# An attention, router and gated-MLP kernel: exponentials and split remainders issued at another point of the attention tick

## The chip, the cores and the metric

The kernel runs on one core of a Trainium2 chip. The metric is the device time of one execution in microseconds (us), lower is better. Three runs of the kernel before took 2026.89 to 2027.23 us, their median is 2026.97 us.

## What is computed

The reference chains three layers; the change lies in the first one.

```python
scores = scale * np.matmul(q, k.transpose(0, 1, 3, 2))
mask = block_i >= block_j
scores = np.where(mask, scores, -1000000000.0)
scores = scores - np.max(scores, axis=-1, keepdims=True)
attn = np.exp(scores)
attn = attn / (np.sum(attn, axis=-1, keepdims=True) + 1e-09)
return np.matmul(attn, v)
...
x = _moe_ref(x=x, **moe_kwargs)
return _moe2_ref(x=x, **moe2_kwargs)
```

q, k and v are (4, 8, 576, 64): four batches of eight heads, 576 positions, 64 channels, with a mask over blocks of 64 positions. Its output, 2304 rows of 512, passes through eight experts with a router that is balanced in eight rounds, and then through a gated layer of width 1536.

## The kernel before, in words

**Pairs and ticks.** Two heads are worked on together, which makes 16 pairs, numbered 0 to 15. Each pair takes eight ticks (u = 0 to 7). A tick handles one piece of the masked score matrix: ticks 0 and 1 hold two row blocks of 64 each, ticks 2 to 5 one block with 320, 384, 448 and 512 columns, and ticks 6 and 7 the two halves (288 columns each) of the last block. So a score tile can be told by its width in the trace. The generator `attention` writes all ticks out in order, and each engine executes its own instructions in exactly that order; an instruction that waits holds up all that stand behind it on its engine or queue.

**One tick.** It has three thirds that end in a `yield`. The first third runs the events that are due in this tick (loads, maxima, scales and splits of coming pairs) and then the score matmuls of the tick (TensorE, L979 and L990). The middle third transposes probabilities that are four ticks old (TensorE, L1068 and L1077), normalises those that are two ticks old (`normalise`: two small VectorE operations that write r, L1035 to L1040, and a product on GpSimd, L1045), copies the transposes out (ScalarE, L1071 and L1078), and takes the row maxima of the tick (`maxima`, VectorE, L1003, which write bias). The last third does the value product at u = 4 and its copy to xf (ScalarE, L1110), the remaining transpose at u = 3, and then the exponentials of the tick before (`exps`, ScalarE, L1020, which write e and need bias).

At each `yield` the caller may put in a step of other work: the loading and splitting of expert weights (wr, w; L372, L377, L179, L183) and, after pair 3, the first part of the expert layer (`fill`: TensorE matmuls of L548 and L614 and their copies). That work fills TensorE beside attention.

**Splitting q and k.** From pair 4 on q and k are split into two float16 parts. For pair p, with r = 8p the tick at which it starts, `load_qk` (L911) brings q (i = 0) and k (i = 1) in, `max_qk` (L924) and `scale_qk` find a power of two, `hi_qk` (ScalarE, L941) writes the upper part into hl at ticks r - 6 (q) and r - 4 (k), and `lo_qk` (VectorE, L945) writes the remainder into hl at ticks r - 5 and r - 4. `lo_qk` also issues eight transfers on SyncE's queue (SP) from hl into st, four for q (L956) and four for k (L958). The scores of the pair's first tick need all eight.

**Buffers.** There is one buffer for q and one for k (qk). `load_qk` of pair p + 1 stands at ticks r - 6 and r - 5, so it waits on SP for the remainders of pair p, which are the last to read the buffer. Score tiles rotate through three PSUM banks, which the exponentials free.

Of the kernel before, what the change touches and what calls it, by code (L numbers as in the profile page):

```python
# [30 lines left out]
def attention_moe_glu_kernel(  # L31
# [74 lines left out]
    def across_mid(g):  # L106
        bank, g["free"] = spread[0](g["name"])
        n = g["n"]
        g["row"] = bank[:, : n * P].rearrange("p (n q) -> p n q", n=n)
        nc.tensor.matmul(  # L110
            bank[:, : n * P], ones, g["d"].rearrange("p n q -> p (n q)"), start=True, stop=True
        )
# [401 lines left out]
    behind = deque()  # L514
# [314 lines left out]
    NTK = len(TICKS)  # L829
# [5 lines left out]
    def attention(actx):  # L835
# [29 lines left out]
        def where(p):  # L865
            return p // NPAIR, ORDER[p % NPAIR]
# [3 lines left out]
        def load_v(b, hp, tag, bufs=1):  # L870
            t = tag
            if isinstance(tag, str):
                t = ap.tile([P, NJ, P], F32, tag=tag, name=f"{tag}_{b}_{hp}", bufs=bufs)
            cols = slice(hp * P, (hp + 1) * P)
            nc.gpsimd.memset(t[S - nf * P :, nf], 0.0)
            nc.sync.dma_start(t[:, :nf], v[b, : nf * P, cols].rearrange("(j p) d -> p j d", p=P))
            nc.sync.dma_start(t[: S - nf * P, nf], v[b, nf * P :, cols])
            return t
# [64 lines left out]
        def lo_qk(p, i):  # L943
            hl = st[p]["hl", i]
            nc.vector.scalar_tensor_tensor(  # L945
                hl[:, 1], qk.pop((p, i)), st[p]["s"][:, i : i + 1], hl[:, 0], op0=ALU.mult, op1=ALU.subtract
            )
            shape = [P, 2, S] if i == 0 else [P, 2, 2, S]
            t = ap.tile(shape, F16, tag=f"st{i}", name=f"st{i}_{p}", bufs=2)
            st[p]["qs" if i == 0 else "ks"] = t  # L950
            for h in range(2):
                a = slice(h * D, (h + 1) * D)
                for half in range(2):
                    d = slice(half * D, (half + 1) * D)
                    if i == 0:
                        nc.sync.dma_start(t[d, h], hl[a, half])  # L956
                    else:
                        nc.sync.dma_start(t[d, h], hl[a])  # L958

        def scores(p, u):  # L960
            g = st[p]
            if u == 0:
                for x in ("bias", "sum", "r"):
                    g[x] = small.tile([P, NC + 1], F32, tag=x, name=f"{x}_{p}")
            if (p, u) in shared:
                sp = shared.pop((p, u))
            elif u == NTK - 1:
                sp = ps_x.tile([P, 512], F32, tag="x", name=f"s_{p}_{u}")
            else:
                sp = ps_s.tile([P, 512], F32, tag="s", name=f"s_{p}_{u}")  # L970
            col, places = 0, []
            for c, k0, k1 in TICKS[u]:
                ps = sp[:, col : col + k1 - k0]
                col += k1 - k0
                places.append((c, k0, k1, ps, c if k0 == 0 else NC))
                if p < DIRECT:
                    for h in range(2):
                        a = slice(h * D, (h + 1) * D)
                        nc.tensor.matmul(  # L979
                            ps[h * CB : (h + 1) * CB],  # L980
                            g["q"][a, c * CB : (c + 1) * CB],
                            g["k"][a, k0:k1],
                            start=True,
                            stop=True,
                        )
                    continue
                qs, ks = g["qs"], g["ks"]
                for i in range(2):
                    for h in range(2):
                        nc.tensor.matmul(  # L990
                            ps[h * CB : (h + 1) * CB],
                            qs[:, h, c * CB : (c + 1) * CB],
                            ks[:, h, i, k0:k1],
                            start=i == 0,
                            stop=i == 1,
                        )
            g["places", u] = places

        def maxima(p, u):
            g = st[p]  # L1000
            for c, k0, k1, ps, m in g["places", u]:
                k, to = k1 - k0, NC if u == NTK - 2 else c
                nc.vector.tensor_tensor_reduce(  # L1003
                    junk[:, :k],
                    ps,
                    zero.to_broadcast([P, k]),
                    g["nsc"],
                    g["bias"][:, NC : NC + 1] if u == NTK - 1 else 3.0e38,
                    ALU.add,
                    ALU.min,  # L1010
                    g["bias"][:, to : to + 1],
                )

        def exps(p, u):
            if u == NTK - 2:
                return
            g = st[p]
            for w in (u,) if u < NTK - 1 else (u - 1, u):
                for c, k0, k1, ps, m in g.pop(("places", w)):
                    nc.scalar.activation(  # L1020
                        et[c][:, k0:k1],
                        ps,
                        AF.Exp,
                        bias=g["bias"][:, c : c + 1],
                        scale=g["sc"],
                        accum_out=g["sum"][:, m : m + 1],
                    )
# [134 lines left out]
        def work(n):  # L1162
            for _ in range(min(n, len(pend))):
                pend.popleft()()

        def hurried():
            if hurry[0]:
                work(1)
                hurry[0] -= 1
                if not hurry[0]:  # L1170
                    ready[0] += S // 2

        events = {}

        def at(tick, f, *a):
            events.setdefault(tick, []).append(lambda: f(*a))

        for p in range(1, npairs):
            r = p * NTK
            if p < DIRECT:  # L1180
                if p > 1:
                    at(r - NTK, load_direct, p)
                    at(r - 2, lambda p: vt.update({p: load_v(*where(p), "v", 2)}), p)
                continue
            for i in range(2):
                if p > 1:
                    at(r - 14 + 1 * i, load_qk, p, i)
                at(r - 11 + i, max_qk, p, i)
                at(r - 6 + 2 * i, hi_qk, p, i)
                at(r - 5 + 1 * i, lo_qk, p, i)  # L1190
            at(r - 8, lambda p: across_mid(st[p]["m"]), p)
            at(r - 7, scale_qk, p)
            at(r - 2, lambda p: vt.update({p: load_v(*where(p), "v", 2)}), p)
        for b in range(B):
            r = (b - 1) * NPAIR * NTK
# [4 lines left out]
            r = r + NPAIR * NTK if b else NPAIR  # L1200
# [13 lines left out]
        def on(k):  # L1214
            return 0 <= k < tot

        for tk in range(tot + NTK):
            p, u = divmod(tk, NTK)
            calm[0] = 0 < u < 5
            here[0] = (p, u) if on(tk) else None  # L1220
            for f in events.pop(tk, ()):
                f()
            here[0] = None
            if on(tk):
                scores(p, u)
            if u == 6 and p < npairs:
                take(p, 0, values(p, 0))
            hurried()
            yield
            out1 = None  # L1230
            if on(tk - 4):
                out1 = transposes(*divmod(tk - 4, NTK))
            if hurry[0]:
                hurried()
            else:
                work(2 if len(pend) > 6 else 1)
            if on(tk - 2):
                normalise(*divmod(tk - 2, NTK))
            if out1:
                out1()  # L1240
            if on(tk):
                maxima(p, u)
            yield

            if p and u == 4:
                work(len(pend))
                take(p - 1, 1, values(p - 1, 1))
                st.pop(p - 1)
                vt.pop(p - 1)
                if p == npairs:  # L1250
                    work(len(pend))
                    ready[0] = B * S // 2
                elif p % NPAIR == 0:
                    hurry[0] = len(pend)
            if p and u == 3:
                rest(p - 1)()
            if on(tk - 1):
                exps(*divmod(tk - 1, NTK))
            if u != 4:
                hurried()  # L1260
            yield
# [647 lines left out]
```

## Time and profile before

| | |
|---|---|
| median of three runs | 2026.97 us |
| profiled execution | 2023.13 us, of which the span is 2021.3 us |
| TensorE busy | 1939.9 us (96%) |
| VectorE, ScalarE, GpSimd busy | 1587.4, 1400.9, 637.2 us |
| attention | from the start to about 345 us of the span |

Times in rows are microseconds from the span's start. PE is TensorE's matmul, PEld its weight load, DVE is VectorE, ACT is ScalarE, POOL is GpSimd, SPq is SyncE's queue of DMA issues. A row of the timeline gives start, length, engine, source line, operation, tiles and count; in square brackets stands how long the engine was idle before it, and what ended that. In a row of waits stand the waiting engine, tile and line, whom it waited for, the sum in us, how often, and the longest.

### The profile page before, as it was taken

What the parts mean: (1) busy time and instruction counts of PE and PEld (TensorE: products, weight loads), DVE (VectorE), ACT (ScalarE), POOL (GpSimd) and SP (SyncE); (2) the same over time, 40 slices, a digit from 0 to 9 for tenths busy, and PEclk for the clock granted to TensorE, in tenths of its full rate; (3) what the DMA queues carried; (4) which work ended last, traced back from release to release, by engine and by line L of the source; (5) the groups of instructions that cost most, each with busy time, mean ns of one, the idle gap of its engine ahead of it and who ended that gap; (6) DMA issues with size and microseconds to landing.
All of it is one profiled execution on the core that took longest, in us unless ns stands there. A gap on an engine that the chain in (4) does not pass through costs nothing. (4 is left out here: it accounts for less than half of the span.)

```text
span 2021.3 us, 47085 instructions
## 1 busy us (share of the span) xinstructions
PE 1939.9 (96%) x18378; PEld 1668.1 (83%) x18378; DVE 1587.4 (79%) x3360; ACT 1400.9 (69%) x2911; POOL 637.2 (32%) x904
## 2 busy tenths in 40 slices
PE   7789999999999999999999999999999989999998
PEld 3457677889888988878888898898889878888987
DVE  8986774888889788797978889788886787677766
ACT  6766775477777778777877877778776666544443
POOL 5644444013333333333333333333332342000000
PEclk9899999999999999999999999999999999999999
DMA  5333331327787786777767767777787200301112
GB/s 154 110 111 111 110 89 39 135 55 140 150 178 157 146 172 130 167 154 162 169 135 164 155 142 173 136 162 156 148 174 167 58 23 17 95 1 45 41 43 53
DMA packets 169615, 238.82 MB, mean 118 GB/s; under 512 B 16688, under 2 KB 85424, under 8 KB 169392
## 3 DMA queue, kind: packets, MB, share of 16 engines
q0 software_dynamic: 68288, 110.39, 31.6%
q1 hardware_dynamic: 100528, 124.90, 19.9%
q8 instruction: 144, 2.36, 0.5%
q14 instruction: 79, 0.65, 0.1%
q10 hardware_dynamic: 576, 0.53, 0.1%
HBM read 90.39 MB, written 24.38 MB: 57 GB/s over the span
## 5 line engine op out<-in xcount | busy, mean ns | idle before, releaser
L548 PEld LDWEIGHTS <-w 128*128 128x128 f16 x6720 | 607.4, 98 | 81.8 <-issue 18.4
L658 PEld LDWEIGHTS <-m_h 128*128 128x128 f16 x5292 | 513.8, 98 | 70.5 <-issue 6.8
L1538 POOL DMA_DIRECT2D acc<-ev x362 | 317.0, 924 | 585.8 <-ACT ev L1542 398.6
L548 PE MATMUL abc_m_b<-xs,w 128*128 128x256 f16 (+1 forms) x3840 | 472.5, 262 | 8.9 <-ACT m_t L575 5.3
L658 PE MATMUL m_o_b<-w,m_h 128*128 128x256 f16 x3024 | 404.3, 273 | 10.0 <-ACT ev L1542 6.1
L658 PE MATMUL m_o_ac<-w,m_h 128*128 128x256 f16 x2268 | 310.4, 273 | 0.0
L548 PE MATMUL abc_m_c<-xs,w 128*128 128x256 f16 (+1 forms) x1920 | 227.2, 262 | 0.0
L1542 ACT ACTIVATE ev<-m_o_b,pe 128x256 f32<-128x256 f32 x370 | 170.8, 479 | 70.7 <-PE m_o_b L658 49.3
L1542 ACT ACTIVATE ev<-m_o_ac,pe 128x256 f32<-128x256 f32 x236 | 136.2, 580 | 44.4 <-PE m_o_ac L658 43.0
L183 DVE SCALAR_TENSOR_TENSOR w<-wr,ws,w 128x512 f16<-128x512 f32 x210 | 156.0, 752 | 8.3 <-ACT w L179 8.3
L179 ACT ACTIVATE w<-wr,ws 128x512 f16<-128x512 f32 x210 | 150.1, 723 | 17.5 <-DVE ws L164 11.9
L194 DVE TENSOR_TENSOR m_h<-m_t,m_h 128x512 f16<-128x512 f32 x189 | 129.5, 686 | 34.3 <-ACT m_h L698 33.3
L698 ACT CAST m_h<-m_t 128x512 f16<-128x512 f32 x189 | 117.2, 620 | 26.6 <-DVE m_t L722 25.5
L691 ACT ACTIVATE m_h<-m_t 128x512 f16<-128x512 f32 x189 | 118.5, 627 | 22.4 <-DVE m_t L587 14.7
L1525 POOL DMA_DIRECT2D acc<-ev_s x52 | 62.1, 1194 | 222.1 <-ACT ev_s L1518 213.8
L695 DVE SCALAR_TENSOR_TENSOR m_h<-m_t,m_h 128x512 f16<-128x512 f32 x189 | 129.0, 687 | 3.1 <-ACT m_h L691 2.8
L548 PEld LDWEIGHTS <-gg_w 128*128 128x128 f16 x1260 | 114.3, 98 | 19.8 <-issue 7.7
L548 PEld LDWEIGHTS <-gv_w 128*128 128x128 f16 x1260 | 114.7, 98 | 15.2 <-issue 3.3
L1045 POOL TENSOR_SCALAR e<-e,r 128x64 f32<-128x64 f32 (+2 forms) x144 | 85.5, 600 | 120.1 <-DVE r L1040 84.5
L658 PEld LDWEIGHTS <-g_h 128*128 128x128 f16 x1134 | 110.5, 98 | 14.8 <-issue 1.9
L548 PE MATMUL abc_m_a<-xs,w 128*128 128x256 f16 (+1 forms) x960 | 118.7, 263 | 0.0
L1732 POOL TENSOR_TENSOR g_t<-v_t,g_t 128x512 f32<-128x512 f32 (+1 forms) x15 | 17.5, 1164 | 280.2 <-DVE v_t L572 239.7
(319 smaller groups left out, 3435.2 us busy)
## 6 DMA issues: line engine op xcount, KB each, us to landing
acc<-ev POOLq DMA_DIRECT2D x362, 256.0 KB, 4.1
wr<-in_w_dram SPq DMA_DIRECT2D x128, 256.0 KB, 5.4
acc<-ev_s POOLq DMA_DIRECT2D x52, 256.0 KB, 3.9
st<-hl SPq DMA_DIRECT2D x48, 144.0 KB, 3.4
raw_g<-in_w_gate_dram SPq DMA_DIRECT2D x12, 512.0 KB, 5.2
raw_v<-in_w_val_dram SPq DMA_DIRECT2D x12, 512.0 KB, 4.9
raw_o<-in_w_out_dram SPq DMA_DIRECT2D x12, 512.0 KB, 5.3
scr_g<-gg SPq DMA_DIRECT2D x21, 256.0 KB, 2.7
```

The lines of the kernel that those rows point to most:

```text
L179: nc.scalar.activation(hi, src, AF.Copy, scale=s)
L183: nc.vector.scalar_tensor_tensor(lo, src, s, hi, op0=ALU.mult, op1=ALU.subtract)
L194: nc.vector.tensor_sub(lo, src, hi)
L548: nc.tensor.matmul(ps[:, f, to : to + w], W[o][:, sh, k, f * P : (f + 1) * P], xs[:, o, mh, k, c0 : c0 + w], start=x not in begun, stop=Tr ...
L658: nc.tensor.matmul(ps, h[o][:, sh, k, ii * P : (ii + 1) * P], W[o][:, mh, k], start=o in (X11, X12) and k == 0 and j == 0, stop=True, skip ...
L691: nc.scalar.activation(hi, src, AF.Relu)
L695: nc.vector.scalar_tensor_tensor(lo, src, 0.0, hi, op0=ALU.max, op1=ALU.subtract)
L698: nc.scalar.copy(hi, src)
L1045: nc.gpsimd.tensor_scalar(et[c][:, :n], et[c][:, :n], g["r"][:, c : c + 1], 1.0, op0=ALU.mult, op1=ALU.mult)
L1525: nc.gpsimd.dma_start(acc[:, x - 1 : x + 1, cols], e, accum_op=ALU.add)
L1538: nc.gpsimd.dma_start(acc[:, x], e, accum_op=ALU.add)
L1542: nc.scalar.activation(e[:, cols], ps, AF.Copy, scale=p)
```

## The change

Two groups of calls are issued at another point of the tick. The exponentials of the tick before now stand at the end of the middle third, behind the row maxima, instead of in the last third. The remainders `lo_qk` stand at the end of the middle third of their tick, behind the row maxima and ahead of the exponentials, instead of among the events of its first third. No operation is added or left out.

```diff
-        events = {}
+        events, behind = {}, {}
...
                 at(r - 11 + i, max_qk, p, i)
                 at(r - 6 + 2 * i, hi_qk, p, i)
-                at(r - 5 + 1 * i, lo_qk, p, i)
+                behind.setdefault(r - 5 + i, []).append(lambda p=p, i=i: lo_qk(p, i))
...
             if on(tk):
                 maxima(p, u)
+            for f in behind.pop(tk, ()):
+                f()
+            if on(tk - 1):
+                exps(*divmod(tk - 1, NTK))
             yield
...
             if p and u == 3:
                 rest(p - 1)()
-            if on(tk - 1):
-                exps(*divmod(tk - 1, NTK))
             if u != 4:
                 hurried()
             yield
```

TensorE and GpSimd keep their order. Three places show what moves on the others.

VectorE, ticks 3 and 4 of pair 8, before (L945 writes the remainders of pair 9, the ISA rows are row maxima):

```order
L945 SCALAR_TENSOR_TENSOR hl_9_2404<-qk_9_2024,qk_s,hl_9_2404 128x576
L116 TENSOR_REDUCE v_r<-v_a 128x1
...
L1003 ISA junk,bias_2304<-s_3_2463,zero,sc_1980 128x384
L1003 ISA bias_2304 128x1
L945 SCALAR_TENSOR_TENSOR hl_9_2512<-qk_9_2056,qk_s,hl_9_2512 128x576
L1039 TENSOR_SCALAR r_2306<-sum_2305 128x1
L1040 RECIPROCAL r_2306<-r_2306 128x1
L1003 ISA junk,bias_2304<-s_4_2520,zero,sc_1980 128x448
```

and with the change:

```order
L116 TENSOR_REDUCE v_r<-v_a 128x1
...
L1003 ISA junk,bias_2304<-s_3_2457,zero,sc_1980 128x384
L1003 ISA bias_2304 128x1
L945 SCALAR_TENSOR_TENSOR hl_9_2404<-qk_9_2024,qk_s,hl_9_2404 128x576
L1039 TENSOR_SCALAR r_2306<-sum_2305 128x1
L1040 RECIPROCAL r_2306<-r_2306 128x1
L1003 ISA junk,bias_2304<-s_4_2514,zero,sc_1980 128x448
L1003 ISA bias_2304 128x1
L945 SCALAR_TENSOR_TENSOR hl_9_2512<-qk_9_2050,qk_s,hl_9_2512 128x576
```

Both remainders moved behind the row maxima of their tick.

SyncE's queue at the same place, before (qk_10 are the loads of pair 10, st_9 the transfers of pair 9, vs a load of v, y a store of the expert layer):

```order
L911 DMA qk_10_2406<-in_qT_dram 128x576
L1403 DMA y_86<-y_2373 128x512
L956 DMA st_9_2438<-hl_9_2404 64x576 x4
L911 DMA qk_10_2443<-in_kT_dram 128x576
L876 DMA vs_0_2459<-in_v_dram 128x4x128
L877 DMA vs_0_2459<-in_v_dram 64x128
L958 DMA st_9_2515<-hl_9_2512 64x1152 x4
```

and with the change:

```order
L911 DMA qk_10_2406<-in_qT_dram 128x576
L1405 DMA y_86<-y_2373 128x512
L911 DMA qk_10_2437<-in_kT_dram 128x576
L876 DMA vs_0_2453<-in_v_dram 128x4x128
L877 DMA vs_0_2453<-in_v_dram 64x128
L956 DMA st_9_2489<-hl_9_2404 64x576 x4
L958 DMA st_9_2530<-hl_9_2512 64x1152 x4
```

The load of the next pair's k, which waits for this pair's second remainder, now stands ahead of the four transfers of q. It is so at each of the eleven pairs 4 to 14; after pair 15 nothing is loaded.

ScalarE, ticks 2 to 5 of pair 1, before (e are exponentials, told by their width; w an expert weight; xf the copy of the value product):

```order
L1078 COPY a_0_278<-t_7_381 128x4x128
L179 ACTIVATE w_0_0_392<-wr_0_00_211,ws_0_371 128x512
L1078 COPY a_0_278<-t_r 128x128
L1020 ACTIVATE e_135,sum_323<-s_2_359,bias_322 128x320
L179 ACTIVATE w_0_1_401<-wr_0_10_215,ws_0_371 128x512
L1071 COPY a_1_403<-t_0_404 128x256
L1110 ACTIVATE xf_0_1_423<-x_1_412,vs_255 128x320
L1020 ACTIVATE e_137,sum_323<-s_3_378,bias_322 128x384
```

and with the change:

```order
L1078 COPY a_0_278<-t_7_381 128x4x128
L1020 ACTIVATE e_135,sum_323<-s_2_359,bias_322 128x320
L179 ACTIVATE w_0_0_393<-wr_0_00_212,ws_0_371 128x512
L1078 COPY a_0_278<-t_r 128x128
L179 ACTIVATE w_0_1_401<-wr_0_10_216,ws_0_371 128x512
L1071 COPY a_1_403<-t_0_404 128x256
L1020 ACTIVATE e_137,sum_323<-s_3_378,bias_322 128x384
L1110 ACTIVATE xf_0_1_424<-x_1_413,vs_255 128x320
```

The exponentials of 320 and 384 columns passed the instructions that stood between the copy of the transposes and them.

## Rows read from the trace of the kernel before

**Rows 1.** The page, busy time by engine.

```profile
PE 1939.9 (96%) x18378; PEld 1668.1 (83%) x18378; DVE 1587.4 (79%) x3360; ACT 1400.9 (69%) x2911; POOL 637.2 (32%) x904
```

**Rows 2.** Windows: stretch, length, busy time of each engine, PEclk, DMA share, GB/s.

```profile
0.00:56.00 56.00, 44.27 (x291) 22.03 (x292) 46.63 (x180) 36.43 (x107) 29.70 (x76) 1.00 0.48 144
56.00:150.00 94.00, 75.65 (x601) 47.09 (x600) 83.10 (x278) 67.25 (x175) 49.06 (x100) 0.89 0.39 112
150.00:345.00 195.00, 188.99 (x1761) 137.76 (x1760) 128.87 (x472) 130.59 (x347) 90.37 (x200) 1.00 0.32 91
```

**Rows 3.** Waits of DVE from 56 to 150 us: sum, times, longest.

```profile
DVE hl L945 <- ACT hl L941: 1.7, 2, 1.5
DVE w_(0, 1)_1828 L183 <- ACT w_(0, 1)_1828 L179: 1.2, 1, 1.2
```

**Rows 4.** Waits of DVE from 150 to 345 us.

```profile
DVE hl L945 <- ACT hl L941: 17.3, 8, 3.9
```

**Rows 5.** Waits of DVE from 0 to 56 us.

```profile
DVE r L1039 <- ACT e L1020: 2.4, 2, 1.4
```

**Rows 6.** Timeline of PE, score tile of tick 4 of pair 10.

```profile
216.53 0.57 PE L990 MATMUL s<-st,st 128*64 128x448 f16 x4 [0.80 <-ACT e L1020]
```

**Rows 7.** Timeline of SPq and DVE around the transfers of pair 4.

```profile
62.03 0.35 SPq L911 DMA_DIRECT2D qk<-in_kT_dram  x1
62.18 0.60 DVE L1003 CUSTOM_DVE_ANT_0 junk<-s,zero 128x448 bf16<-128x448 f32 x1
...
64.85 2.42 SPq L372 DMA_DIRECT2D wr<-in_w_dram  x4
...
69.87 0.68 DVE L377 TENSOR_REDUCE wmx<-wr 128x1 f32<-128x512 f32 x1
```

**Rows 8.** Tile wr, issue to landing: loads at 64.85, then at 109.03.

```profile
DMA to landing us min/median/max: 3.8/4.4/4.9
...
DMA to landing us min/median/max: 3.4/4.6/4.7
```

**Rows 9.** Timeline of SPq and DVE around the transfers of pair 6.

```profile
104.84 0.67 DVE L1003 CUSTOM_DVE_ANT_0 junk<-s,zero,sc 128x448 bf16<-128x448 f32 x1
...
106.59 2.39 SPq L958 DMA_DIRECT2D st<-hl  x4
109.03 2.52 SPq L372 DMA_DIRECT2D wr<-in_w_dram  x4
...
112.67 0.68 DVE L377 TENSOR_REDUCE wmx<-wr 128x1 f32<-128x512 f32 x1
```

**Rows 10.** Timeline of SPq, DVE and PE around the transfers of pair 9.

```profile
176.78 2.40 SPq L956 DMA_DIRECT2D st<-hl  x4
...
181.28 0.82 DVE L945 SCALAR_TENSOR_TENSOR hl<-qk,qk_s,hl 128x576 f16<-128x576 f32 x1 [3.85 <-ACT hl L941]
...
183.55 2.73 SPq L958 DMA_DIRECT2D st<-hl  x4
...
189.73 0.36 PE L990 MATMUL qk_a<-st,st 128*64 128x64 f16 x7 [0.33 <-DMA st<-hl]
```

**Rows 11.** Tile st, pair 9: issues (ns min/median/max, first and last start), landing.

```profile
L958 SPq DMA_DIRECT2D st<-hl x4: 587/602/807, 183.6 to 185.7; - x4
...
DMA to landing us min/median/max: 3.2/3.9/4.0
```

**Rows 12.** Timeline of PE, first scores of pair 13.

```profile
276.25 0.36 PE L990 MATMUL qk_a<-st,st 128*64 128x64 f16 x8
```

**Rows 13.** Tile st, pair 13: issues and landing, as in rows 11.

```profile
L958 SPq DMA_DIRECT2D st<-hl x4: 461/600/606, 269.4 to 271.2; - x4
...
DMA to landing us min/median/max: 3.5/3.9/4.0
```

**Rows 14.** Waits of PE from 56 to 150 us.

```profile
PE t L1077 <- POOL e L1045: 6.8, 4, 2.3
PE s L990 <- ACT e L1020: 6.5, 4, 2.6
```

## Prediction

> **What bounds the kernel now.** I read the page first: TensorE is busy for 96% of the span [rows 1], so a change can only win what TensorE loses somewhere, and attention is where it loses it. The busy times by stretch [rows 2] cut attention into three stages. From 0 to 56 us and from 56 to 150 us VectorE sets the pace: it is busy for 46.6 of 56 us and 83.1 of 94 us, while TensorE has 11.7 and 18.4 us idle. From 150 to 345 us TensorE sets the pace: 189.0 of 195 us busy, 6 us idle, VectorE at 128.9. So I count in two currencies. In the first two stages a microsecond counts if VectorE loses or gains it; in the third, if TensorE does. After 345 us nothing is moved, and the work left over is TensorE's, so what attention gains or loses goes into the end.
>
> Next I read who waits for whom on these two engines, and then the timeline of SyncE's queue beside it, since the moved remainders issue transfers.
>
> **What the change takes away.** PE's and POOL's orders stay as they are, and no operation comes or goes. Four waits can shrink.
>
> First, a remainder waits on VectorE for its upper part, which ScalarE writes in the same tick. In the second stage that is 1.7 us [rows 3]. Behind the row maxima the upper part has a third of a tick more, so I take all 1.7. The 17.3 us of the third stage [rows 4] I cost at nothing: TensorE's own work covers them, and they would count only if VectorE became the bound there.
>
> Second, the normalisation waits on VectorE for exponentials, 2.4 us in the first stage [rows 5]. There the exponentials of 320 and 384 columns pass an expert weight and the copy xf, so I take all 2.4.
>
> Third, in the second stage VectorE waits 1.2 us for an upper half of an expert weight [rows 3]. ScalarE reaches it sooner, because the exponentials of 384 columns now run while it would be waiting for the value product. I take 1.2.
>
> Fourth, in the third stage TensorE waits 0.8 us for exponentials to free a score bank [rows 6]; those pass a step of expert work. I take 0.8.
>
> The sum is 1.7 + 2.4 + 1.2 + 0.8 = 6.1 us. The lower bound of each is zero: an in-order engine that skips one wait may meet the next.
>
> **What the change adds.** The remainders issue eight transfers, and their place on SyncE's queue changes with them. The load of the next pair's k stands at the head of that queue until the second remainder has been read; the four transfers of q were ahead of it and are now behind it. Those four take 2.40 us of the queue [rows 10], which before ran in the wait between the two remainders. So the transfers of k, and what follows them, come 2.4 us later, plus whatever the second remainder itself is late. I follow it where something is waiting.
>
> Pair 4. The load of k went out at 62.03, right behind the second remainder. That remainder now ends where the row maxima ended before, since it leaves their front and goes to their back: 62.18 + 0.60 and about 0.1 for the read-out, 62.8. Then come the load (0.35), 2.4 and 2.4 for the eight transfers, and the four expert-weight loads start at 68.1 in place of 64.85, 3.2 us later [rows 7]. The shortest landing of those four was 3.8 us [rows 8], so the first was there at about 68.7, and VectorE read it at 69.87 [rows 7], 1.2 us later. 3.2 - 1.2 = 2.0 us of VectorE. With the longest landing, 4.9 us, nothing of the slack is left and it is 3.1. I take 2.0, because the first of four loads meets the least company.
>
> Pair 6. The maxima of tick 4 end at 104.84 + 0.67 = 105.5, and there the second remainder ends now. With 0.4 for the load and 4.8 for the transfers the weight loads start at 110.7 in place of 109.03, 1.7 us later [rows 9]. With the shortest landing, 3.4 us [rows 8], the slack before VectorE's read at 112.67 was 0.2. That leaves 1.5 us.
>
> The first scores of pairs 4 to 6 will also find their transfers late, and there TensorE waits, but VectorE, which sets the pace, comes to their maxima some microseconds after. I cost these at nothing; if that cover fails it is up to 1 us for each of the three.
>
> Pair 9, in the third stage. The second remainder is bound by the upper part, not by its place: it waited 3.85 us for it [rows 10], and the maxima that now go ahead fit into that wait. So it is not late, and the shift is the 2.4 us of q's transfers alone. The last of k's transfers was issued at 185.7 and the longest landing was 4.0 us [rows 11], which gives 189.7, and the scores started at 189.73 after a wait for just that [rows 10]. No slack: 2.4 us of TensorE.
>
> Pair 13. The last issue at 271.2 and 4.0 us to land [rows 13] give 275.2. The scores started at 276.25 [rows 12], a slack of 1.05: 2.4 - 1.05 = 1.35 us of TensorE.
>
> The other pairs of the third stage leave more between last issue and scores. I put them at zero, and keep up to 1 us for each of pairs 10, 11, 14 and 15.
>
> The sum is 2.0 + 1.5 + 2.4 + 1.35 = 7.25 us.
>
> On the landing the trace and the notes differ. The transfers of k, 144 KB each, took 3.2 to 4.0 us at pair 9 [rows 11]. The Trainium skill, "DMA: Bandwidth & Descriptors", section "Anatomy of one DMA", fits 2.0 us and bytes at 436 GB/s for a transfer that GpSimd issues, which for these would be an estimate of 2.3 us. By that, 1.7 us more slack, pair 13 would lose nothing, pair 9 about 0.7, the weights about 0.8 and 0.7, and the whole change would come out at about -3.9 us. The measured landing decides, and the sum stays on it.
>
> **Sum.** -6.1 + 7.25 = +1.15 us. Against the profiled execution's 2023.1 us that is 2024.3; the median of the runs lies 3.8 us above that execution, so I forecast **2028.1 us**, no change. With the gains halved or the losses halved, the forecast itself runs from 2024.5 to 2031.2. A difference of 0.2%, 4 us, is about what a measurement of this kernel can tell from no change.
>
> **The rivals.**
>
> *Late transfers everywhere (slower).* The load of k at the head of the queue delays the scores at all pairs of the third stage, not at two. The price is 2.4 + 1.35 for pairs 9 and 13 and 1 us each for the four others, 7.75, with 3.5 for the weights, and only half the gains, 3.0: +8.2 us, 2035. It decides from the point where the last transfer of k is issued less than about 6.4 us before the scores (4.0 us to land and the shift of 2.4). For it: pair 9 already waited for such a transfer. Against it: in every other pair there was no wait at all for them. Every such gap also sits in the stage in which the granted clock was 1.00, full 2.4 GHz; in the stage before, with TensorE busy for 80%, it was 0.89 [rows 2], which means that some of it ran at 1.2 GHz. A gap that takes the clock down would add to the price.
>
> *The exponentials are the chain (faster).* In the second stage TensorE waits 6.8 us for normalised rows and 6.5 us for exponentials [rows 14]. If these chains, and not VectorE's work, set the pace there, then earlier exponentials shorten them, by half at a guess: -6.6 us on top, 2021.5. For it: those 13.3 us are most of TensorE's 18.4 idle. Against it: VectorE is busy for 88% of that stage, and the waits for exponentials of the pair's first tick, whose neighbours on ScalarE do not change, cannot shrink.
>
> *The exponentials do not start sooner.* They need the row maxima of their tick, and where VectorE is a tick behind, ScalarE would only stand at them longer. Then the second, third and fourth gains, 4.4 us, are gone: +5.55 us, 2032.5.
>
> **How the numbers follow.** The forecast has 0.44. The first rival has 0.24 and the third 0.07, both slower: 0.31. The faster rival has 0.25, since the gains are bounded less well than the losses. The range from 2019 to 2038 takes in all four cases with their bounds and leaves out the far ends of the two outer ones.
>
> **What would show it.** Right, if VectorE's wait for the upper part (L945 on L941) is gone nearly everywhere; if its normalisation no longer waits in the first stage; if SyncE issues the transfers of q only behind the load of k, with all eight in one run; if the first scores of pair 9 wait about 2.7 us for st, and those of pair 13 about 1.3; and if VectorE's maximum of the expert weights (L377) waits for a load at about 70 and 113 us. Wrong, if the first scores of the third stage wait at more than two pairs (first rival), or if TensorE's idle time between 56 and 150 us falls by more than 5 us (second rival), or if ScalarE's waits for bias grow by several microseconds (third).

## The result and the profile after

The change made the kernel slower: 2035.78 us, the median of ten runs, against 2026.93 for ten runs of the kernel before beside them, a ratio of 1.0055 (95% 1.0043 to 1.0066). One slow run of before, 2238.09 us, doesn't count in the ratio; the two medians alone would make 1.0044. Forecast was no change, 2028.1. The profiled execution of after took 2034.33 us, its span 2032.5.

The page by engine answers to [rows 1], the windows over attention to [rows 2]: in the third stage TensorE is busy for 181.6 of 195 us in place of 189.0, at a clock of 0.98 in place of 1.00. Columns as there.

```profile
PE 1943.6 (96%) x18378; PEld 1671.1 (82%) x18378; DVE 1588.6 (78%) x3360; ACT 1399.6 (69%) x2911; POOL 635.0 (31%) x904
```

```profile
0.00:56.00 56.00, 44.37 (x284) 21.86 (x284) 44.66 (x168) 35.65 (x105) 26.69 (x74) 0.97 0.47 139
56.00:150.00 94.00, 74.93 (x587) 46.60 (x587) 80.70 (x274) 63.66 (x167) 45.75 (x95) 0.89 0.41 114
150.00:345.00 195.00, 181.62 (x1667) 129.99 (x1667) 131.16 (x475) 129.02 (x344) 90.62 (x199) 0.98 0.33 89
```

Where it goes: the scores of 448 columns come once in each pair, so their starts show how late after runs. They are 3.9 us later than before at pairs 7 and 8, 9.3 at pair 9, 9.6 at pair 12, 11.8 at pair 13 and 12.2 at pair 15 (323.18 became 335.37). Kernels below that lose nothing (E1, E6, E7) are 2.0 to 4.4 us behind before's profiled execution at pair 7 as well, so that lateness can't be put down to the change. What these traces place is the 8.3 us from pair 8 to pair 15, and 5.4 + 2.2 of it stand at pairs 9 and 13. The ratio makes 11.1 us of the whole change; where the rest lies, the traces don't show.

Pair 9 in the timeline of after, which answers to [rows 10]; y is a store of the expert layer, and ScalarE (L1373) writes the next y only when it has left the buffer:

```profile
181.39 0.33 SPq L911 DMA_DIRECT2D qk<-in_qT_dram  x1
181.77 0.42 SPq L1405 DMA_DIRECT2D y<-y  x1
...
185.37 0.69 ACT L1373 ACTIVATE y<-abc,iw 128x512 f32<-128x512 f32 x1 [3.44 <-DMA y<-y]
185.96 0.77 ACT L941 ACTIVATE hl<-qk,qk_s 128x576 f16<-128x576 f32 x1
186.76 0.82 DVE L945 SCALAR_TENSOR_TENSOR hl<-qk,qk_s,hl 128x576 f16<-128x576 f32 x1 [3.56 <-ACT hl L941]
187.61 0.33 SPq L911 DMA_DIRECT2D qk<-in_kT_dram  x1
...
189.07 3.37 SPq L956 DMA_DIRECT2D st<-hl  x4
...
191.83 0.75 DVE L924 TENSOR_REDUCE qm<-qk 128x1 f32<-128x576 f32 x1 [1.18 <-DMA qk<-in_kT_dram]
192.49 2.52 SPq L958 DMA_DIRECT2D st<-hl  x4
...
193.26 0.28 PE L1276 MATMUL abc_lg<-wg,xs 128*128 128x16 f16 x5 [0.76 <-DVE r L1039]
...
195.73 0.23 PE L990 MATMUL qk_a<-st,st 128*64 128x64 f16 x1 [1.65 <-DMA st<-hl]
197.20 0.50 PE L990 MATMUL qk_a<-st,st 128*64 128x64 f16 x7 [1.24 <-DMA st<-hl]
197.63 1.46 PE L548 MATMUL abc_m_b<-xs,w 128*128 128x256 f16 x6
```

and the first steps of it before, with the matmuls behind the first scores:

```profile
175.89 0.33 SPq L911 DMA_DIRECT2D qk<-in_qT_dram  x1
176.27 0.42 SPq L1403 DMA_DIRECT2D y<-y  x1
...
179.89 0.69 ACT L1371 ACTIVATE y<-abc,iw 128x512 f32<-128x512 f32 x1 [1.84 <-DMA y<-y]
...
190.02 0.83 PE L548 MATMUL abc_m_b<-xs,w 128*128 128x256 f16 x6
```

Two delays add up. The load of the next q waits at the head of SyncE's queue for this pair's remainder of q. That is later now, so the load and the store of y behind it go out 5.5 us later than before, 1.6 more than the 3.9 by which the pair is late. ScalarE stands 1.60 us longer at the store, and the upper part of k, its remainder and the load of k are all late by the same 5.5. Then q's four transfers take 3.37 us of the queue ahead of k's, which start 8.9 us later. TensorE waits 2.89 us for st in two pieces where it waited 0.33. The late load of k holds VectorE too: its maximum of that k stands for 1.18 us, and TensorE waits 0.76 us for what VectorE writes behind it, before it comes to these scores; in the profile of before neither wait stands there.

So TensorE is idle here for 3.3 us more than before. Behind that its clock falls, and the six matmuls of L548 that follow take 1.46 us in place of 0.83; together the two make nearly all of the 5.4 us. Windows of ten microseconds of after:

```profile
180.00:190.00 10.00, 9.69 (x88) 6.67 (x86) 5.54 (x16) 5.93 (x16) 4.45 (x14) 1.00 0.35 92
190.00:200.00 10.00, 6.12 (x68) 4.43 (x65) 6.04 (x28) 2.54 (x8) 6.02 (x15) 0.72 0.76 199
200.00:210.00 10.00, 10.00 (x84) 6.45 (x84) 5.14 (x20) 9.16 (x26) 3.34 (x6) 0.94 0.11 31
```

Before, PEclk was 1.00 in all three. The waits of VectorE in after, first from 56 to 150 us, then from 150 to 345: the wait for the upper part is gone in the second stage [rows 3] and 7.3 us in place of 17.3 in the third [rows 4]; waits for loads have come.

```profile
DVE wmx L377 <- DMA wr<-in_w_dram: 4.0, 3, 2.5
...
DVE hl L945 <- ACT hl L941: 7.3, 2, 3.8
DVE qm L924 <- DMA qk<-in_qT_dram: 3.4, 3, 1.6
DVE qm L924 <- DMA qk<-in_kT_dram: 1.6, 3, 1.2
```

### The profile page after: what moved, and what is told of

Its sections match the earlier page's. It is cut to its first block, busy times and chain, and to the rows that moved or that the text cites. A ratio compares the mean times of both kernels' runs of the same rounds, so it can differ in the third digit from the quotient of the medians.

```text
span 2032.5 us, 47088 instructions
## 1 busy us (share of the span) xinstructions
PE 1943.6 (96%) x18378; PEld 1671.1 (82%) x18378; DVE 1588.6 (78%) x3360; ACT 1399.6 (69%) x2911; POOL 635.0 (31%) x904
## 5 line engine op out<-in xcount | busy, mean ns | idle before, releaser
L548 PEld LDWEIGHTS <-w 128*128 128x128 f16 x6720 | 609.9, 98 | 81.8 <-issue 17.5
L548 PE MATMUL abc_m_b<-xs,w 128*128 128x256 f16 (+1 forms) x3840 | 476.0, 263 | 7.8 <-ACT m_t L575 4.1
L548 PE MATMUL abc_m_c<-xs,w 128*128 128x256 f16 (+1 forms) x1920 | 227.1, 262 | 0.0
L548 PEld LDWEIGHTS <-gg_w 128*128 128x128 f16 x1260 | 113.8, 98 | 19.7 <-issue 8.1
L548 PEld LDWEIGHTS <-gv_w 128*128 128x128 f16 x1260 | 114.8, 99 | 15.1 <-issue 3.3
L548 PE MATMUL abc_m_a<-xs,w 128*128 128x256 f16 (+1 forms) x960 | 119.3, 264 | 0.0
```

Source lines behind the costliest of these rows:

```text
L548: nc.tensor.matmul(ps[:, f, to : to + w], W[o][:, sh, k, f * P : (f + 1) * P], xs[:, o, mh, k, c0 : c0 + w], start=x not in begun, stop=Tr ...
```

## Experiments: which part costs it

The change has four effects: X, the exponentials; V, the later remainder on VectorE, of q and of k; and Q, the order of SyncE's queue. TensorE's order is that of before in all kernels but E8, E11, E13 and E15. Ratios are to runs of the kernel before on the same chip, with 95% intervals.

**E1, exponentials alone** (X). Diff against after:

```diff
-                behind.setdefault(r - 5 + i, []).append(lambda p=p, i=i: lo_qk(p, i))
+                at(r - 5 + 1 * i, lo_qk, p, i)
```

> Exponentials moved as in the change, remainders and all transfers as before. Queue theory (the loss comes from SyncE's queue, where the load of the next pair's k now stands ahead of the four transfers of q): 0.997 to 1.001, and the first scores of pair 9 wait for st at most 0.5 us. Rival, exponentials (their new place puts them ahead of copies and weights that others need): 1.004 to 1.006. Rival, late remainders (VectorE writes them later, whatever the queue does): 0.997 to 1.001.

Measured 0.9998 (0.9989 to 1.0006). The exponentials neither cost nor bring anything.

**E2, remainders alone** (V and Q): the change without its other move.

```diff
             for f in behind.pop(tk, ()):
                 f()
-            if on(tk - 1):
-                exps(*divmod(tk - 1, NTK))
...
                 rest(p - 1)()
+            if on(tk - 1):
+                exps(*divmod(tk - 1, NTK))
```

> Remainders moved as in the change, with the queue order that follows from it; exponentials as before. Queue theory: 1.004 to 1.007, first scores of pair 9 about 5 us later against those of pair 8 than before. Rival, exponentials: 0.999 to 1.001. Rival, late remainders: 1.004 to 1.007.

Measured 1.0070 (1.0056 to 1.0085): the whole loss is here. The exponentials theory is out. E2 lost more than the change did, though the intervals overlap; in the traces pair 13 makes the difference, 5.0 us against 2.2, and the last section comes back to it.

**E3, the change with the old queue** (X and V).

```diff
-                    at(r - 14 + 1 * i, load_qk, p, i)
+                    if i == 0:
+                        at(r - 14, load_qk, p, i)
+                    else:
+                        behind.setdefault(r - 13, []).append(lambda p=p: load_qk(p, 1))
...
```

> The whole change, but the load of the next pair's k (and three loads of v behind it) is issued behind the first remainder's transfers, so that SyncE's queue has the order of before. Queue theory: 0.997 to 1.001, waits for st in the third stage under 1 us in all. Rival, exponentials: 1.004 to 1.006. Rival, late remainders: 1.004 to 1.006, the waits for st stay.

Measured 1.0028 (1.0017 to 1.0040). Half is gone, half stays: neither theory holds alone.

**E4, the queue alone** (Q): `lo_qk` before, with the four transfers of q as a function of their own.

```diff
+                if i == 0:
+                    behind.setdefault(r - 5, []).append(lambda p=p: st_qk(p, 0))
...
```

> The kernel before in all engines' order; only the four transfers of q are issued behind the row maxima, so that SyncE's queue has the order of the change. Queue theory: 1.004 to 1.006. Rival, exponentials: 0.999 to 1.001. Rival, late remainders: 0.999 to 1.001.

Measured 1.0029 (1.0019 to 1.0039), short of the 1.004 to 1.006 that the queue theory gave for the whole loss, and above the rivals' 1.001: the queue makes about half. The timeline of pair 9 in E4:

```profile
191.52 0.19 PE L995 MATMUL qk_a<-st,st 128*64 128x64 f16 x1 [0.36 <-DMA st<-hl]
193.06 0.34 PE L995 MATMUL qk_a<-st,st 128*64 128x64 f16 x7 [1.34 <-DMA st<-hl]
```

**E7, the remainder of k alone; E9, the remainder of q alone**, both with the old queue (in E9 by E3's loads) and the old exponentials.

```diff
                 if i == 0:
                     at(r - 5, lo_qk, p, 0)
                 else:
+                    behind.setdefault(r - 4, []).append(lambda p=p: lo_qk(p, 1))
```

> The kernel before, but the remainder of k alone is issued behind the row maxima; SyncE's queue keeps its order. Theory (in the third stage k's remainder is bound by its upper part, and it is the remainder of q that holds up the store of y): 1.000 to 1.002, with what it costs in the second stage. Rival (k's remainder is the late one, its transfers are the last that the scores need): 1.002 to 1.004, and the wait of pair 9's first scores for st grows by over 1 us.

Measured 0.9999 (0.9991 to 1.0008).

```diff
                 if i:
                     at(r - 4, lo_qk, p, 1)
                 else:
+                    behind.setdefault(r - 5, []).append(lambda p=p: lo_qk(p, 0))
```

> The kernel before, but the remainder of q alone is issued behind the row maxima, and the load of the next pair's k behind its transfers, so that SyncE's queue keeps its order; exponentials and k's remainder as before. Theory (q's later remainder holds the load of the next q at the head of SyncE's queue, with a store of y behind it, and ScalarE waits for that store ahead of the upper part of k): 1.002 to 1.004, ScalarE's wait for the store at pair 9 over 3 us in place of 1.84, and that pair's first scores about 1.5 us later. Rival (q's and k's remainders together cost it, VectorE's time behind the maxima): 1.000 to 1.001.

Measured 1.0039 (1.0027 to 1.0051). So V is q's remainder alone: its 0.39% and Q's 0.29% make 0.68%, and E2 lost 0.70%, within the intervals. In E9's timeline ScalarE waits at the store as in after:

```profile
185.31 0.69 ACT L1382 ACTIVATE y<-abc,iw 128x512 f32<-128x512 f32 x1 [3.41 <-DMA y<-y]
```

## Experiments: how q's remainder and the queue cost it

**E5, the change with both loads behind their remainders; E6, the same on the kernel before.** In `lo_qk`, ahead of the transfers:

```diff
+            if p + 1 < npairs:
+                load_qk(p + 1, i)
...
-                if p > 1:
+                if p == DIRECT:
...
```

> The whole change, but each load of the next pair's q and k is issued right behind the remainder that frees its buffer, ahead of that remainder's transfers, instead of up to a tick earlier; so no load waits at the head of SyncE's queue and the stores of y pass it. Theory (all of the loss comes through SyncE's queue: a load that waits for a remainder holds up the transfers of q in one case and a store of y in the other, and ScalarE waits for that store ahead of the upper part of k): 0.997 to 1.001; at pair 9 ScalarE waits for the store of y for under 1 us, and the first scores for st for at most 0.6 us. Rival (remainders that VectorE writes later are late by themselves): 1.002 to 1.004, with waits for st of over 1 us at pair 9.

> The kernel before with the same move of the loads alone. Theory: the store of y goes out sooner, so the 1.84 us for which ScalarE waited at pair 9 go away and nothing else does: 0.998 to 1.000. Rival (the loads are later and the maxima of q and k wait for them): 1.001 to 1.003.

E5 measured 1.0016 (1.0008 to 1.0025), E6 1.0005 (0.9995 to 1.0014). In the third stage of E5 ScalarE has no wait for the store of y left and TensorE none for st, and some 70% of the loss are gone; but not all, and the time is above the theory's 0.997 to 1.001. E6 gains nothing: the 1.84 us on ScalarE before were covered.

**E10, E9 with the load of q behind too.**

```diff
-                    if i == 0:
-                        at(r - 14, load_qk, p, i)
+                    if p == DIRECT:
+                        at(r - 14 + 1 * i, load_qk, p, i)
...
+                        behind.setdefault(r - 13, []).append(lambda p=p, i=i: load_qk(p, i))
```

> As with q's remainder alone, but the load of the next pair's q is issued behind the transfers of q too, so that the store of y passes it. Theory: the loss goes, 0.999 to 1.001, and ScalarE's wait for the store of y at pair 9 is under 1 us. Rival: as with q's remainder alone, whatever that is.

Measured 1.0028 (1.0017 to 1.0039): the time is a miss. The wait for the store is gone, and at pair 9 the scores of 448 columns come 0.6 us earlier against pair 8 (2.9 later in E9), but 3.6 us are lost at pairs 10, 11 and 14. VectorE now waits for the next q, which is loaded into the buffer that the later remainder frees. Two rows of the timeline of E10, ScalarE's y with no wait, and in pair 9 VectorE's maximum of the q that pair 11 needs; and its waits from 150 to 345 us, which before had none for q:

```profile
181.85 0.69 ACT L1382 ACTIVATE y<-abc,iw 128x512 f32<-128x512 f32 x1
...
206.88 0.75 DVE L924 TENSOR_REDUCE qm<-qk 128x1 f32<-128x576 f32 x1 [1.20 <-DMA qk<-in_qT_dram]
```

```profile
DVE qm L924 <- DMA qk<-in_qT_dram: 11.4, 7, 2.7
```

**E12 (on E10) and E14 (on E5), the maximum of q behind the row maxima.**

```diff
-                at(r - 11 + i, max_qk, p, i)
+                if i:
+                    at(r - 10, max_qk, p, 1)
+                else:
+                    behind.setdefault(r - 11, []).append(lambda p=p: max_qk(p, 0))
```

> As with q's remainder alone and the queue freed (ratio 1.0028), and the maximum of the next pair's q is taken behind the row maxima of its tick instead of ahead of them. Theory (what is left of the loss is VectorE standing at that maximum, since the next q is loaded into the buffer that the later remainder frees, 1.2 us at pair 10): 0.9995 to 1.0015, with VectorE's waits for the load of q under 0.5 us from 150 to 345 us. Rival (the remainder's own place on VectorE delays the normalisation): 1.002 to 1.0035.

> The whole change with the loads behind their remainders (ratio 1.0016) and the maximum of q behind the row maxima. If queue, store and maximum are all that the change costs: 0.9985 to 1.0010. Rival (the exponentials or VectorE's order cost something of their own): 1.001 to 1.002.

E12 measured 1.0026 (1.0014 to 1.0037), E14 1.0020 (1.0009 to 1.0031): the theory falls, the time stays. VectorE's waits for the next q are down from 11.4 to 1.2 us in E12 (the theory had under 0.5) and gone in E14. But now it stands at the maximum of the next k, which neither run moved: 2.5 us in E12 and 3.5 in E14, where before had 0.4. E12, its waits from 150 to 345 us and the rows of that maximum:

```profile
DVE qm L924 <- DMA qk<-in_kT_dram: 2.5, 3, 1.4
DVE qm L924 <- DMA qk<-in_qT_dram: 1.2, 3, 0.7
```

```profile
205.43 0.40 SPq L911 DMA_DIRECT2D qk<-in_kT_dram  x1
...
209.12 0.75 DVE L924 TENSOR_REDUCE qm<-qk 128x1 f32<-128x576 f32 x1 [0.48 <-DMA qk<-in_kT_dram]
...
230.25 0.75 DVE L924 TENSOR_REDUCE qm<-qk 128x1 f32<-128x576 f32 x1 [1.43 <-DMA qk<-in_kT_dram]
...
297.57 0.75 DVE L924 TENSOR_REDUCE qm<-qk 128x1 f32<-128x576 f32 x1 [0.55 <-DMA qk<-in_kT_dram]
```

and the first of these loads in before:

```profile
200.35 0.35 SPq L911 DMA_DIRECT2D qk<-in_kT_dram  x1
```

That load goes out 5.1 us later in E12, in a pair that is only 4.2 us late: it stands behind the four transfers of q and the load of q, and these wait for q's remainder. TensorE of E12 loses 0.5 to 0.8 us at each of pairs 10, 11, 13 and 14; just ahead of 10, 11 and 14 stand the three waits. Kernels that lose nothing (E1, E6, E7, E15) have at most 0.3 us of waits for these loads in the third stage. So the traces put what is left of q's remainder, 0.2 to 0.3%, down to these later loads more than to its place on VectorE. That is read and not tested, since no run moved the maximum of k, and pair 13 stays open.

A second buffer for q and k, which would part load from remainder, wasn't tried.

## Experiments: what a gap of TensorE costs

**E8, E2 with its two gaps filled** by work that the kernel doesn't need.

```diff
+                if u == 0 and col == k1 - k0:
+                    for _ in range({9: 32, 13: 16}.get(p, 0)):
+                        nc.tensor.matmul(sp[:CB, : 3 * CB], st[p - 1]["qs"][:, 0, :CB], ...)
```

> The remainders moved alone (ratio 1.0070), with 32 and 16 extra matmuls of 192 columns ahead of the first scores of pairs 9 and 13, into score columns that are written over; they add work that the kernel doesn't need, some 2.3 and 1.1 us, in gaps of 3.7 and 1.6 us. Theory (a gap of TensorE costs its own length and about as much again, since TensorE runs at 1.2 GHz behind it: about 3.4 us behind each): granted clock 1.00 in every ten microseconds from 160 to 345, ratio 1.003 to 1.0045. Rival (the lower clock is not due to the gap, or costs nothing): 1.006 to 1.008.

Measured 1.0032 (1.0020 to 1.0044). Adding matmuls took back more than half of E2's loss. Windows of E2 and then of E8, from 190 and from 280 us:

```profile
190.00:200.00 10.00, 6.04 (x69) 4.36 (x70) 6.69 (x30) 3.25 (x9) 6.20 (x15) 0.79 0.78 218
200.00:210.00 10.00, 10.00 (x78) 6.54 (x78) 4.94 (x22) 8.60 (x24) 3.34 (x6) 0.87 0.07 20
...
280.00:290.00 10.00, 7.64 (x86) 5.24 (x85) 7.84 (x29) 5.91 (x17) 6.38 (x15) 0.89 0.67 173
290.00:300.00 10.00, 10.00 (x71) 6.94 (x70) 4.69 (x21) 7.41 (x21) 2.50 (x6) 0.76 0.01 3
```

```profile
190.00:200.00 10.00, 8.86 (x117) 7.28 (x114) 6.18 (x28) 4.09 (x12) 6.08 (x15) 1.00 0.73 194
200.00:210.00 10.00, 10.00 (x86) 6.49 (x85) 6.37 (x22) 8.42 (x25) 4.17 (x8) 1.00 0.22 63
...
280.00:290.00 10.00, 9.08 (x113) 6.76 (x109) 6.99 (x33) 5.47 (x17) 6.23 (x15) 1.00 0.59 159
290.00:300.00 10.00, 10.00 (x89) 6.63 (x89) 6.58 (x22) 8.41 (x24) 4.28 (x9) 1.00 0.26 75
```

Pair 9 costs 3.2 us in place of 5.6 and pair 13 2.4 in place of 5.0, by the starts of the scores of 448 columns. Those scores get their transfers as late as in E2, to within 0.3 us; what is saved, 2.4 and 2.6 us, is the stretch at 1.2 GHz behind each gap, about as much again as what stays.

**E11, the second stage filled,** on the kernel before: there TensorE waits 2.3, 1.9 and 1.9 us for normalised rows behind the scores of 384 columns.

```diff
+            if u == 3 and p in (4, 5, 6):
+                for _ in range(28):
+                    nc.tensor.matmul(sp[:CB, 3 * P :], g["qs"][:, 0, :CB], g["ks"][:, 0, 0, :P], ...)
```

> The kernel before with 28 extra matmuls of 128 columns behind the scores of 384 columns of pairs 4, 5 and 6, into score columns that nothing reads; they add work that the kernel doesn't need, some 2 us each time, in the gaps of 2.3, 1.9 and 1.9 us in which TensorE waits for normalised rows. If TensorE's clock counts in the second stage (a gap there is followed by some 3 us of work at 1.2 GHz): 0.996 to 0.9985, and the granted clock of 56 to 150 us rises from 0.89 to 0.95 or more. Rival (VectorE sets the pace there, as the prediction has it, and TensorE only gets more idle time): 0.9990 to 1.0010, with the clock up.

Measured 0.9973 (0.9964 to 0.9982), 2019.64 us: faster than both kernels. The second stage in E11, and the transposes that end the first gap, before and in E11 (the 28 matmuls in between):

```profile
56.00:150.00 94.00, 78.57 (x699) 52.55 (x699) 83.87 (x281) 68.13 (x179) 50.76 (x103) 0.95 0.41 115
```

```profile
75.41 1.11 PE L1077 MATMUL t<-ident,e 128*128 128x128 f32 x4 [2.32 <-POOL e L1045]
```

```profile
72.91 1.73 PE L1000 MATMUL s<-st,st 128*64 128x128 f16 x28
75.41 0.66 PE L1086 MATMUL t<-ident,e 128*128 128x128 f32 x4 [0.78 <-POOL e L1054]
```

**E13, more filling,** ahead of the scores of 384 columns too, into columns of the score tile before.

> The kernel before with the extra matmuls that gave 0.9973, and 16 or 32 more of 192 columns ahead of the scores of 384 columns of pairs 4 to 7, where TensorE waited 1.3, 1.7, 0.9 and 2.6 us for a score bank. If each of these gaps is still followed by work at 1.2 GHz: 0.995 to 0.997 and the granted clock of 56 to 150 us at 0.98 or more. Rival (the first filling has taken what there was): 0.9965 to 0.9985.

Measured 1.0064 (1.0050 to 1.0078), a miss that tells nothing of the question: the new matmuls waited for the row maxima of the tile into which they write.

```profile
77.40 2.40 PE L973 MATMUL s<-st,st 128*64 128x192 f16 x14 [6.12 <-DVE bias L1023]
```

**E15, the change without q's remainder, and E11's filling.**

> The change without its one costly part: the exponentials and the remainder of k moved, the remainder of q where it was, SyncE's order as before; and with the 28 extra matmuls behind the scores of 384 columns of pairs 4 to 6 that gave the kernel before 0.9973. If exponentials and k's remainder cost nothing together either: 0.9960 to 0.9985. Rival (together they cost VectorE or ScalarE something in the third stage): 0.9990 to 1.0010.

Measured 0.9974 (0.9966 to 0.9983), 2018.71 us, as E11. Exponentials and k's remainder cost nothing together either; q's remainder and the order of SyncE's queue are the parts of the change that do.

## Why the prediction was wrong

**The remainder of q is the step that failed.** The prediction wrote of pair 9 that the second remainder "is bound by the upper part, not by its place" and "is not late". The first holds: k's remainder moved alone costs nothing (E7, 0.9999). The second doesn't, since it took the upper part's time as given. ScalarE writes that part behind a wait for the store of y, the store stands behind the next q's load, and that waits for the first remainder; so the second one came 1.6 us later against the pair. The order of SyncE's queue ahead of the prediction has the store between the load and the transfers; only the transfers were followed. For the four transfers of q 2.4 us were priced and for q's remainder nothing; E9 puts the latter at 0.39%, some 8 us. At pair 9 the path through the store is shown: 2.9 us are lost there in E9 and none in E10. In the kernel's time it is not clear of noise: E10's 1.0028 lies within the interval of E9's 1.0039. E10 loses 3.6 us at pairs 10, 11 and 14, where VectorE waits for the later loads, a path that the prediction didn't have either.

**The gap was priced at its length.** The wait for st at pair 9 was forecast as 2.7 us and was 2.89, at pair 13 1.35 and was 1.56. That these come so near is luck. At pair 9 the last of k's transfers was issued 4.8 us later against the pair and not 2.4 (194.4 for 185.7, less 3.9), it landed sooner than [rows 11] had it, and TensorE itself came later, by the 0.76 us for which it had waited for VectorE. The pair cost 5.4 us, since this wait and the lower clock came on top. That a gap could take the clock down stood in a rival, unpriced; E8 prices it at 2.4 and 2.6 us, behind waits of 3.7 and 1.6 us in E2. Pair 13 in after kept its clock at 1.00 and cost 2.2.

**The queue's term was right in kind.** E4 gives 0.29%, 5.9 us. Its trace places 3.1 us at pair 9 and 0.5 at pair 13, together near the 3.75 that were forecast for the two, but the parts were off in opposite directions: the clock behind the gap was left out, and the wait itself was taken too long. At pair 9 it grew by 1.37 us in E4 and not by 2.4, as the transfers of k land sooner there, in 2.5 to 2.7 us where before had 3.2 to 4.0 [rows 11]. So they do in after:

```profile
DMA to landing us min/median/max: 2.4/2.5/2.6
```

From the Trainium skill, "DMA: Bandwidth & Descriptors", "Anatomy of one DMA", the prediction had worked out an estimate of 2.3 us for these transfers, by a fit for those that GpSimd issues. The traces of E4 and after come close to it, and that of before doesn't. So [rows 11], taken in the old order, was no price for the new one. Why they land sooner isn't shown; in the old order k's transfers stand right behind two loads of v, in the new one q's four stand between.

**The gains were not there.** Of 6.1 us E1 shows none in the time. In after the wait for the upper part, 1.7 us, is gone from the second stage; the wait for the weight went from 1.2 to 1.0 us; the score bank at pair 10 still costs 0.80 us, the same as in [rows 6]. The wait for the normalisation in the first stage went from 2.4 to 1.6 us, and there VectorE met the next wait, as the lower bound of zero allowed: its row maxima wait 3.8 us for scores in place of 0.9.

**The second stage was read wrongly.** VectorE did wait for the weights, 4.0 us against 3.5 forecast, yet at pair 7 after is 3.9 us late where E6 and E7, which lose nothing, are 3.6 and 4.4. TensorE is idle for 18 us there but works at 1.2 GHz for part of the rest, and E11 shows that it counts: clock 0.95 in place of 0.89, 0.27% faster with no work taken from VectorE. Whether the first stage was read rightly no run shows. A clock under 1.00 in [rows 2] was the hint that busy time alone does not tell who sets the pace.

**The rivals.** 2035 us was named by "late transfers everywhere", and its time is near. Its mechanism is not what happened: apart from pairs 9 and 13 the only wait for st of the third stage is 0.23 us, at pair 11, which meets its sign of more than two pairs by the letter but not its price of 1 us for each of four others. Exponentials as the chain are out by E1. That exponentials bring no gain is what the third rival said, and E1 agrees; but its reason doesn't show, as ScalarE's waits for bias grow by 0.9 us in the first stage and 0.5 in the second, and the loss has other causes.

## What to carry to other kernels

Before moving an instruction that is the last reader of a single buffer, follow its refill: the refill waits at the head of a DMA queue, and everything behind it there moves too, up to an engine that waits for a store, and to whoever reads the refill next. Price a gap of TensorE by the clock behind it as well as by its length. Where the granted clock of a stretch is under 1.00, ask what fills its gaps before calling another engine the bound.

## Not expected of the hardware

Short gaps were enough for work at 1.2 GHz behind them: in E4 PEclk is 0.83 from 190 to 200 us behind waits of 0.36 and 1.34, and before, behind a wait of 2.32, four transposes took 1.11 us that took 0.66 in E11. It did not follow each time: at pair 13 of after, waits of 0.22, 0.27 and 1.29 us left the clock at 1.00, while in E2 nearly the same waits there, 0.26, 0.22 and 1.34, were followed by 0.89 and 0.76 and cost 2.7 us more. What decides between the two is not shown. The windows of after, where E2 has its rows above:

```profile
280.00:290.00 10.00, 7.61 (x93) 5.58 (x90) 8.23 (x32) 5.64 (x16) 6.42 (x15) 1.00 0.67 175
290.00:300.00 10.00, 9.92 (x90) 6.52 (x87) 5.46 (x23) 9.14 (x27) 3.34 (x6) 1.00 0.13 40
```

Matmuls whose results nobody reads made the kernel 0.27% faster.
